# Top-32 attention and a squared-ReLU feed-forward on one core: 30 more idle products on TensorE, and new orders of the engines

## The chip, the cores and the metric

The kernel runs on one core of a Trainium2 chip. The metric is device time in microseconds (us) of one execution; less is better. The core has five engines with a queue each: TensorE (PE in the rows, PEld for its weight loads), VectorE (DVE), ScalarE (ACT), GpSimd (POOL) and SyncE (SP), which only issues DMAs here. Each executes its queue in order, and engines wait for each other by semaphores.

## What is computed

Eight batches, eight heads, 576 rows of 64. Each row of scores keeps its 32 largest entries, the rest get no weight; then a softmax and the product with v. The result, as 4608 rows of 512, goes through two products with a squared ReLU between them.

```python
scores = scale * np.matmul(q, k.transpose(0, 1, 3, 2))          # 8 x 8 x 576 x 576
kth = np.partition(scores, -top_k, axis=-1)[..., -top_k:-top_k + 1]   # top_k = 32
scores = np.where(scores >= kth, scores, -1000000000.0)
attn = np.exp(scores - np.max(scores, axis=-1, keepdims=True))
attn = attn / (np.sum(attn, axis=-1, keepdims=True) + 1e-09)
x = np.matmul(attn, v)            # then heads side by side: 4608 x 512
h = x @ w_in                      # 512 x 2048
g = np.maximum(h, 0.0) ** 2
out = g @ w_out                   # 2048 x 512
```

## The kernel before

The work is cut into 144 groups. A group is 128 rows of a pair of heads (or the last 64 rows of two pairs, the Z groups). Each goes through the same stages:

- TensorE multiplies q and k (`scores`, L870 in the rows, because all plain products go through one helper `mm`; transposes go through `tr`, L873). q and k were flipped before by five transposes each (`turned_`), and ScalarE copied them out of PSUM (L996).
- ScalarE copies the scores from PSUM to the tile `s` (`copied`, L1040), and VectorE folds them from PSUM (`fold`, L1118, three per group) into a list that holds the larger ones. GpSimd makes the complementary lists by two integer sums (`whole`, L1113).
- VectorE finds the threshold of each row by MAX8 and MATCH_REPLACE8 (L1165, L1180, L1160, L1183 for `kth`); for 71 of the groups ScalarE and GpSimd do a part of it (L1170, L1173).
- ScalarE makes the mask from `s` and `kth` (L1206, one activation for each of the two heads). TensorE turns the scores by transposes and adds the masks by products (`flip`: `turn`, then `mask`), and ScalarE exponentiates out of PSUM (`grow`, L1272).
- TensorE multiplies with v (`fav`, L1338), ScalarE drains it (L1375), GpSimd divides by the row sums (L1384), SP flips the result by DMA.
- For each chunk of 256 or 128 rows TensorE makes h (`fh`), ScalarE applies ReLU (L1430), GpSimd or ScalarE squares (L1445, L1448), TensorE multiplies with w_out (`fo`), ScalarE copies out (L1466) and SP stores.

GpSimd also issues 14 DMAs (`issue`, L1658 to L1660) that copy v, half a batch each, to a bf16 copy `vd` in memory; a 1x1 memset follows each. Loads of v for batches after the first read `vd`.

PSUM has eight banks: two areas of three (`large`: flips of q and k, scores, turns) and two single ones (`psum`: products with v, h, out, and idle products). Whoever takes an area waits until the last reader of its former content is done.

Two kinds of idle work are in TensorE's queue. An idle product (`t` in `times`, `fill=True`) multiplies a block of ones with 512 columns of ones into a `psum` bank; nobody reads it. A spare (`spare`, a negative number in the order) is three products of 128 columns added into an area that is about to be overwritten or read elsewhere.

The program makes all operations in a list, numbered as they are made, and `Plan.arrange` then puts them into an order written out by hand: `ORDER` has one string of numbers for each engine, and `SLOT` one digit for each tile, its place in its pool. Numbers below 89 are set-up, weight loads and casts and GpSimd's DMA issues (61, 63, ... 87); 89 to 2534 are idle products, of which the order names only a few; the rest follow from the groups. The semaphore waits follow from the order and the places.

```python
turns = {e: [int(x) for x in orders[e].split()] for e in ENGS}
place = {ops[x]: i for e in ENGS for i, x in enumerate(turns[e]) if x >= 0}
for t, s in zip(tiles, slots):
    if t.taker in place:
        t.slot = int(s)
```

Of the kernel before, what the change touches and what calls it, by code (L numbers as in the profile page):

```python
# [32 lines left out]
        "90 91 92 93 94 95 96 97 98 2541 2542 2543 2547 2574 2579 101 100 104 106 102 2613 2614 2617 2645 126 119 129 134 2683 136 135 2684 2577 2687 2750 "  # L33
        "2751 257 149 245 169 2605 2715 2607 2643 2754 209 3221 3222 274 2672 2783 153 2674 2713 2865 275 -5029 -5029 -5029 -5029 -5029 -5029 -5029 -5029 183 "
        "-5029 2895 240 283 2742 -5137 2924 -5041 2744 2781 210 2954 3286 3287 292 2810 2983 2891 294 2812 3017 2922 244 3048 190 148 3354 3355 241 204 2893 "
        "2950 3076 2952 -5157 219 2981 3107 3009 2817 276 2818 2820 2821 3135 3011 3419 3420 2824 2825 2827 2828 3044 3224 293 207 -5203 -5203 3252 256 278 "
        "2831 2838 2832 2839 3074 2841 2842 226 3289 3103 2834 2835 -5232 3046 -5232 -5232 3317 3133 2845 188 2848 2846 167 3357 3105 2847 2852 3162 2849 2851 "
        "2850 222 3164 3250 3385 3279 2855 2859 2856 2860 3422 3281 3315 2858 2857 3170 3450 3171 3344 2862 3173 3174 3532 3920 3921 3177 2861 3178 3562 3383 "
        "3184 3346 3185 3591 3180 195 3412 3181 3191 3192 3414 3448 3621 3187 3188 3985 3986 3194 -5409 3195 3650 3477 3198 3200 3201 3684 4053 4054 3205 "
        "-5409 3199 159 3204 3479 3558 3715 3589 3202 3560 3203 3743 3208 3210 3209 3212 3213 3617 3214 3215 3211 3648 3774 3619 3802 3491 3492 3484 3485 4118 "  # L40
        "3487 3488 3676 4119 3505 3494 3923 3506 3495 3711 3498 3508 3509 3499 3951 3678 3741 3501 3512 3514 3502 3988 3515 3713 3770 3519 3518 4016 3800 3513 "
        "3516 3772 3517 3829 4056 4084 3522 3525 3831 3526 3528 3949 3529 3978 3524 4588 4589 4121 3980 4014 3527 3523 3837 3838 4149 3840 3841 4043 3844 3845 "
        "3851 4045 4231 4082 3847 3852 3848 4261 4111 3854 3855 4290 3885 4113 4653 3887 3858 3888 3886 3859 4147 3890 3896 4654 3897 3891 4321 3892 3893 4176 "
        "3898 3899 3901 3903 3902 3904 4350 4384 3861 3862 3865 3866 4721 4178 4722 3867 3868 4257 4415 3870 4259 3869 3871 3875 3876 3877 4288 3881 3878 3872 "
        "4317 4443 3880 3882 4348 3879 3907 3909 4474 4786 4787 3910 3908 4319 4376 4502 3913 4378 3914 3912 3911 4411 4591 4183 4184 4441 4186 4187 4413 4619 "
        "4470 4190 4191 4656 4472 4500 4193 4197 4194 4198 4684 4204 4205 4200 4201 4724 4529 4207 4208 4211 4213 4752 4531 4212 4789 4221 4223 4214 4617 4215 "
        "4216 4228 4222 4218 4646 4227 4217 4682 4817 4225 4899 4226 4224 4537 4538 4540 4541 4544 4545 4711 4648 4929 4551 5287 5288 4552 4547 4548 4958 4558 "
        "4554 4555 4559 4750 4561 4562 4713 4779 4988 5352 4781 5353 4565 4566 4815 5017 4572 5420 5421 4571 4567 4844 5051 4925 4846 4568 4569 4570 4927 4956 "
        "5082 4575 5110 4577 4579 4582 4581 4578 4984 5141 4576 4580 5015 4986 4858 4859 5169 4851 4852 5043 4865 4866 4854 4855 5290 5485 5486 5045 4861 4862 "
        "5078 4872 4868 5318 4869 5108 4873 4875 4876 5355 5080 5137 4879 4881 4880 5383 4884 5139 5167 4882 4883 4885 4886 5196 5423 5316 5198 4889 4892 4894 "  # L50
        "5451 5955 5956 4890 4893 4896 4891 5345 5488 4895 5347 5381 5204 5205 5207 5516 5211 5208 5212 5598 5218 5219 5214 5215 5410 5221 5252 5254 5222 5253 "
        "5255 5628 5225 5226 5263 5264 5265 5266 5449 5257 5260 5258 5259 5412 5657 5478 5268 5269 5271 5228 5229 5270 5687 5242 5961 5962 5480 5243 5246 5716 "
        "5245 5248 5514 5244 5232 5249 5238 5543 5750 5237 5235 5997 5234 5247 5998 5239 5781 5233 5236 5624 5545 5274 5281 5810 5655 5278 5626 5279 5683 6003 "
        "6004 5841 5714 5685 5280 5277 5869 5276 5275 5742 5550 5551 5553 5554 5964 5744 5777 5564 5565 5557 5558 6006 5567 5808 5560 5561 6073 5568 5779 5837 "
        "5571 5572 5574 5575 6101 5867 5578 5579 5839 5580 6132 5581 5896 5582 5585 5584 5583 5588 5593 5595 5898 6160 5990 5594 5590 5591 5589 5592 6033 6194 "
        "5992 6656 6035 6657 5904 5905 5911 6099 6222 5907 5908 5912 6128 5914 5915 5918 6253 6130 6281 5919 5921 5922 6158 5925 5926 5928 5929 6363 6187 6041 "
        "6044 5932 6043 5934 5938 5935 6042 6391 5933 5939 6189 5936 5937 6422 6220 5942 5948 6046 5944 6047 5947 6048 6049 6450 6249 5945 5943 5946 5949 6251 "
        "6279 6662 6663 6052 6054 6055 6053 6484 6057 6059 6308 6060 6058 6063 6066 6512 6310 6065 6389 6064 6068 6543 6698 6699 6070 6069 6067 6418 6571 6704 "
        "6705 6420 6665 6448 6322 6323 6325 6707 6315 6326 6316 6477 6318 6319 6329 6742 6330 6510 6479 6332 6333 6772 6539 6336 6337 6339 6340 6806 6541 6353 "
        "6569 6343 6344 6348 6349 6347 6350 6346 6345 6836 6358 6598 6359 6354 6357 6355 6600 6691 6902 6734 6356 6360 6693 7385 7386 6932 6736 6966 6605 6606 "  # L60
        "6608 6609 6768 6612 6613 6615 6616 6799 6996 6770 6619 6620 7062 6801 6626 6627 6622 6623 6832 6629 6630 6633 6863 7092 6834 6634 6635 6636 6637 6640 "
        "6639 6638 6865 7126 6928 6643 6648 6649 6645 6644 6647 6930 6959 7156 6650 6646 6992 6961 6870 6871 6873 6872 6875 6877 6878 6876 7222 7023 6881 6884 "
        "6883 6886 6888 6889 6882 6887 7252 6994 7391 7392 6892 7025 6893 6898 7088 7286 6899 7428 7429 6894 6897 6896 6895 7316 7119 7090 7434 7435 7152 7394 "
        "7121 7030 7183 7031 7033 7035 7032 7038 7036 7037 7437 7041 7154 7044 7043 7248 7046 7048 7042 7049 7047 7504 7052 7055 7185 7053 7054 7250 7279 7534 "
        "7057 7281 7312 7058 7056 7059 7568 7343 7190 7193 7191 7192 7598 7314 7345 7421 7201 7203 7195 7196 7197 7198 7202 7204 7664 7206 7207 7208 7209 7212 "
        "7214 7213 7423 7215 7350 7352 7351 7353 7464 7694 7217 7466 7219 7216 7355 7218 7357 7358 7356 7530 7728 7361 7532 7362 7364 7363 7366 7368 7369 7367 "
# [1764 lines left out]
```

## Time and profile before

| | us |
|---|---|
| median of 3 runs (lowest, highest) | 744.44 (744.16, 746.62) |
| profiled execution | 745.29 |
| its span, first to last instruction | 743.5 |
| VectorE busy | 718.7 |
| ScalarE busy | 714.8 |
| TensorE busy with products | 698.1 |
| GpSimd busy | 685.1 |

The span is what the profiler saw from the first to the last instruction of the execution; the time lies 1.79 us above it. A busy time is the sum of what one engine executed, so the span less the busy time is what that engine idled in all. A mean granted clock of TensorE of 0.994 says that it was at its full level nearly throughout.

### The profile page before, as it was taken

The page shows a single profiled execution, that of the slowest core. Times are in us where ns is not written, and L with a number is a line of the kernel's source. Part 1 is how long each engine was busy: PE and PEld are TensorE (multiplying, and loading weights), DVE is VectorE, ACT ScalarE, POOL GpSimd, SP SyncE. Part 2 cuts the span into 40 slices and gives each one's busy share as a digit, 9 for nine tenths or more (in the row PEclk, how much of TensorE's full clock was granted, in tenths as well). Part 3 has the DMA queues.
Part 4 walks back from the last instruction along what each step waited for, and adds up shares of the span by engine and source line. Part 5 has one row for each costly group of instructions (what it writes and reads, how often), then busy time and mean ns, then how long its engine had stood idle before and what let it go on. Part 6 is the DMA issues. An engine that isn't in the chain of part 4 may idle for free.

```text
span 743.5 us, 27477 instructions
## 1 busy us (share of the span) xinstructions
PE 698.1 (94%) x10556; PEld 524.8 (71%) x10626; DVE 718.7 (97%) x3409; ACT 714.8 (96%) x1202; POOL 685.1 (92%) x526
## 2 busy tenths in 40 slices
PE   7787999999899999999999999999999999999997
PEld 3555766767677677767778677677677777777786
DVE  5999999999999999999999999999999999999996
ACT  4799999999999999999999999999999999999994
POOL 3799999999999999899999999999999999999981
PEclk9899999999999999999999999999999999999999
DMA  8765553354324441224332352204633032301101
GB/s 177 175 162 125 139 142 82 71 80 98 56 70 75 84 83 27 63 56 78 71 64 56 76 119 46 55 13 89 127 74 85 12 68 54 59 20 45 30 26 50
DMA packets 172729, 57.30 MB, mean 77 GB/s; under 512 B 157744, under 2 KB 164912, under 8 KB 172592
## 3 DMA queue, kind: packets, MB, share of 16 engines
q1 hardware_dynamic: 164528, 51.19, 29.8%
q0 software_dynamic: 7392, 4.13, 4.7%
q8 instruction: 84, 1.38, 0.8%
q14 instruction: 53, 0.43, 0.2%
q10 hardware_dynamic: 672, 0.16, 0.1%
HBM read 40.83 MB, written 13.57 MB: 73 GB/s over the span
## 4 chain that ended last, share of the span: by engine, by line
ACT 44%; PE 26%; DVE 19%; POOL 5%; issue 4%; DMA 1%; SPq 0%; ACTq 0%; POOLq 0%; DVEq 0%
PE ps L870 21%; ACT w L1206 12%; ACT s L1040 9%; ACT p L1272 9%; PE ps L873 6%; ACT g L1430 5%; DVE s L1118 4%; DVE s L1180 4%; DVE c L1165 4%; ACT s L1170 4%; DVE kth L1183 3%; DVE s L1160 3%; ACT qk L996 3%; POOL u L1113 2%; POOL s L1113 2%
## 5 line engine op out<-in xcount | busy, mean ns | idle before, releaser
L1113 POOL TENSOR_TENSOR u<-s 128x864 int32<-128x864 int32 x142 | 244.7, 1724 | 20.3 <-DVE s L1118 18.2
L1113 POOL TENSOR_TENSOR s<-s,u 128x864 int32<-128x864 int32 x142 | 242.8, 1714 | 3.5
L1206 ACT ACTIVATE w<-s,kth 128x576 bf16<-128x576 f32 x286 | 224.0, 834 | 1.9 <-DVE kth L1183 1.8
L1165 DVE MAX8 c<-s 128x8 f32<-128x140 f32 (+2 forms) x864 | 203.7, 265 | 0.1
L1118 DVE TENSOR_TENSOR s<-ps,s 128x288 f32<-128x288 f32 x432 | 192.4, 446 | 10.3 <-ACT s L1040 7.8
L870 PE MATMUL ps<-qk 64*128 64x192 f32 (+3 forms) x1280 | 179.7, 428 | 9.5 <-ACT p L1272 4.8
L1180 DVE MATCH_REPLACE8 s<-c,s 128x106 f32<-128x106 f32 (+2 forms) x722 | 181.5, 256 | 0.0
L1040 ACT COPY s<-ps 128x1152 f32<-128x1152 f32 (+1 forms) x145 | 168.2, 1161 | 5.2 <-PE ps L870 4.5
L1272 ACT ACTIVATE p<-ps 128x1152 bf16<-128x1152 f32 x143 | 169.1, 1182 | 3.1 <-PE ps L870 2.6
L870 PEld LDWEIGHTS ps<-qk 64*128 64x128 f32 (+1 forms) x1280 | 131.0, 176 | 38.1 <-ACT p L1272 15.3
L870 PE MATMUL ps<-wo,g 128*128 128x512 bf16 (+1 forms) x522 | 131.5, 373 | 9.1 <-issue 6.7
L870 PE MATMUL ps<-xt,win 128*128 128x256 bf16 (+1 forms) x1280 | 131.3, 252 | 1.3 <-ACT g L1430 0.4
L1183 DVE MAX8 kth<-s 128x8 f32<-128x296 f32 x288 | 129.3, 456 | 0.7 <-POOL s L1173 0.4
L1160 DVE MAX8 s<-s 128x8 f32<-128x288 f32 x288 | 126.5, 448 | 0.2 <-POOL s L1113 0.2
L873 PEld LDWEIGHTS ps<-ident,s 64*128 64x128 f32 x2592 | 95.6, 139 | 42.9 <-ACT w L1206 8.8
L873 PE MATMUL ps<-ident,s 64*128 64x64 f32 x2592 | 111.9, 228 | 11.4 <-ACT qk L996 3.8
L870 PEld LDWEIGHTS ps<-xt,win 128*128 128x128 bf16 x1280 | 98.1, 98 | 21.5 <-issue 4.1
L1445 POOL TENSOR_TENSOR g<-g 128x1024 bf16<-128x1024 bf16 x50 | 94.6, 1895 | 3.2 <-ACT g L1430 2.6
L1430 ACT ACTIVATE g<-ps 128x512 bf16<-128x512 f32 x140 | 86.9, 657 | 0.0
L870 PEld LDWEIGHTS ps<-wo,g 128*128 128x128 bf16 x592 | 48.8, 98 | 46.8 <-issue 5.5
L870 PEld LDWEIGHTS ps<-vb,p 128*128 128x128 bf16 (+1 forms) x1600 | 53.9, 100 | 23.3 <-ACT g L1430 5.1
L870 PE MATMUL ps<-steep_bf,w 64*128 64x64 bf16 x2584 | 66.7, 191 | 0.1
(90 smaller groups left out, 711.5 us busy)
## 6 DMA issues: line engine op xcount, KB each, us to landing
out_dram<-o SPq DMA_DIRECT2D x32, 256.0 KB, 2.3
rk<-in_k_dram SPq DMA_DIRECT2D x63, 128.0 KB, 2.5
rq<-in_q_dram SPq DMA_DIRECT2D x62, 128.0 KB, 2.6
s<-s SPq DMA_DIRECT2D x144, 32.0 KB, 1.9
g<-in_moe_w_in_dram SPq DMA_DIRECT2D x8, 512.0 KB, 4.5
g<-in_moe_w_out_dram SPq DMA_DIRECT2D x8, 512.0 KB, 4.4
vd<-in_v_dram POOLq DMA_DIRECT2D x14, 288.0 KB, 4.8
vb<-vd SPq DMA_DIRECT2D x56, 64.0 KB, 2.3
```

Of the source, the lines that this page charges most:

```text
L870: return pe.matmul(o, l, r, start=start, stop=stop, skip_group_check=True)
L873: return pe.matmul(o, i, ident, is_transpose=True, skip_group_check=True, **kw)
L1040: return pl.op("act", .14 + 2 * (c1 - c0) / 1200, pl.at("copy", tg - LEAD + 1), lambda: act.copy(at(st)[:, :, c0:c1], two(banks(ss)[:, FIR ...
L1113: return pl.op("gp", dur, prio, lambda: gp.tensor_tensor(o().bitcast(I32), x().bitcast(I32), y().bitcast(I32), op), **kw)
L1118: return dve(.36, lambda: vec.tensor_tensor(o(), two(banks(ss)[:, FIRST_AT + c:], SECOND, QUART), x(), ALU.max), r=[ss], **kw)
L1160: prev[i] = [dve(.0685 + HALF / 960, lambda i=i: vec.max(area(LIST, LIST + 8, i), area(LESS, LESS + HALF, i)), after=prev[i] + [low], hold ...
L1165: lambda i=i, t=t, span_=span_: vec.max(eighth(t, i), span_(i)),
L1180: lambda i=i, t=t, span_=span_: vec.match_replace(span_(i), eighth(t, i), span_(i), NEG), hold=[st])]
L1183: ks.append(chain(kth, i, prev[i], .0685 + (8 + HALF) / 960, lambda i=i: vec.max(eighth(kth, i), area(BIGS - QUART, LIST + 8, i)), hold=[st]))
L1206: masks[i:] = [pl.op("act", .77, pl.at("mask", tw + .8 * i), lambda i=i: act.activation(at(wt)[:, i, :], at(st)[:, i, 0:S], ACTF.Relu, bia ...
L1272: return act.activation(at(pt)[:, :, :].rearrange("p c (h q) -> p h c q", h=2), bass.AP(x.tensor, x.offset, [x.ap[0], [APART, 2], [64, 9], ...
L1430: return act.activation(at(g)[:, g0:g0 + 512], bank(hh)[:, 0:512], ACTF.Relu)
```

## The change

All of it is in the two constants. The order of TensorE names 81 idle products instead of 51: numbers 103, 105, 107 to 118, 120 to 125, 127, 128, 130 to 133, 137 and 138 within the first part, 89 and 99 far back. Some of the old ones (169, 183, 209, 244, 153, 148 and others) stand elsewhere. One spare of three products is replaced by another. Of the other operations the same ones are named: 557 of TensorE's 1128, 431 of ScalarE's 1059, 2309 of VectorE's 2687 and 184 of GpSimd's 508 stand at another place (by up to 14, 10, 45 and 14 places). GpSimd's DMA issues are among them: 63 stands ahead of 2693 (the second integer sum of the fifth group) instead of behind 2666 (a product of L1173); 65, 67 and 69 stand 6, 14 and 10 places earlier, 73 stands 10 later, the others by 1 to 11 in either direction. SP's order is the same. In `SLOT` 266 of 3990 places differ. The searched orders were made with a model that has the traced time of GpSimd's DMA issues; nothing of that model's constants is changed in the file.

In the cut diff, 2574 is the second flip of q, 2579, 2617, 2645, 2687, 2715 and 2754 are scores, 2613 and 2614, 2683 and 2684, 2750 and 2751 flips of q and k, 2577, 2605 and 2643 the first turns, 2607 a product with v.

```diff
@@ -30,191 +30,192 @@
 ORDER = {
     "pe": (
-        "90 91 92 93 94 95 96 97 98 2541 2542 2543 2547 2574 2579 101 100 104 106 102 2613 2614 2617 2645 126 119 129 134 2683 136 135 2684 2577 2687 2750 "
...
+        "90 91 92 93 94 95 96 97 98 2541 2542 2543 2547 2574 137 138 2579 101 100 104 106 102 2613 2614 131 132 133 2617 2645 126 119 129 134 127 128 130 2683 "
+        "136 135 2684 120 121 122 123 124 125 2577 2687 2750 2751 116 117 118 2605 2715 169 2607 183 2643 2754 3221 3222 274 2672 2783 209 2674 244 2713 2865 "
+        "153 148 -5029 -5029 -5029 -5029 -5029 -5029 -5029 -5029 -5029 2895 240 292 2742 111 112 113 114 115 -5041 2924 -5041 257 2744 2781 108 109 110 2954 "
...
+        "6994 7391 7392 6892 7025 6895 6893 7088 7286 6897 7428 7429 6894 6899 6896 6898 7316 7119 7090 89 99 7434 7435 7152 7394 7121 7030 7183 7033 7035 "
...
     "gp": (
-        "2539 1 2 7 5 3 4 6 8 9 11 10 16 25 28 15 13 21 23 26 19 20 22 2611 17 18 12 61 24 27 2576 14 2622 2623 2650 2651 2692 34 2693 2666 63 2720 36 2721 "
...
+        "2539 1 2 7 5 3 4 6 8 9 11 10 16 25 28 15 13 21 23 26 19 20 22 2611 17 18 12 61 24 27 2576 14 2622 2623 2650 2651 2692 34 63 2693 2666 2720 36 2721 "
...
@@ -231,8 +232,8 @@
...
 SLOT = (
-    "01010101010101010010101010010100000000000000001000000000000001010000000000011000000000000000001010000000000000100001000000100000000000101100"
...
+    "01010101010101010010101010010100000000000010001000001000000001010100000000001000000000000000001000000000000000100001010000000000000000100100"
...
```

## Rows read from the trace of the kernel before

**Rows 1.** The page of the profile: span, and busy time of each engine with its share of the span and its instructions.
```profile
span 743.5 us, 27477 instructions
PE 698.1 (94%) x10556; PEld 524.8 (71%) x10626; DVE 718.7 (97%) x3409; ACT 714.8 (96%) x1202; POOL 685.1 (92%) x526
```

**Rows 2.** Busy time by stretch. Columns: start and end, length, then busy us (instructions) of TensorE's products, its weight loads, VectorE, ScalarE and GpSimd, the granted clock, the share of the DMA engines, GB/s.
```profile
20.00:40.00 20.00, 16.35 (x186) 11.82 (x186) 18.35 (x89) 15.87 (x22) 15.46 (x13) 0.83 0.75 173
40.00:720.00 680.00, 648.09 (x9991) 489.40 (x10059) 671.92 (x3204) 676.87 (x1146) 656.84 (x473) 1.00 0.34 73
...
40.00:100.00 60.00, 50.75 (x815) 38.62 (x815) 59.88 (x286) 59.85 (x98) 58.53 (x47) 1.00 0.56 145
...
500.00:720.00 220.00, 213.01 (x3397) 163.32 (x3422) 216.25 (x1039) 218.12 (x376) 212.83 (x156) 1.00 0.27 58
```

**Rows 3.** The same view in steps of 2 us, with the same columns; the granted clock is the third number from the end.
```profile
22.00:24.00 2.00, 0.70 (x25) 0.70 (x26) 2.00 (x9) 1.27 (x2) 1.52 (x2) 1.00 0.93 209
24.00:26.00 2.00, 2.00 (x30) 1.51 (x24) 2.00 (x14) 1.13 (x1) 1.92 (x2) 0.65 1.06 321
26.00:28.00 2.00, 2.00 (x10) 1.51 (x9) 1.89 (x8) 1.83 (x3) 0.84 (x1) 0.50 0.22 48
...
32.00:34.00 2.00, 0.77 (x20) 0.65 (x20) 1.49 (x7) 2.00 (x3) 1.36 (x1) 1.00 1.07 262
34.00:36.00 2.00, 1.69 (x39) 1.69 (x41) 2.00 (x11) 1.59 (x7) 0.88 (x2) 0.71 0.74 160
36.00:38.00 2.00, 2.00 (x9) 1.33 (x6) 1.91 (x8) 1.05 (x2) 2.00 (x3) 0.50 0.86 253
...
52.00:54.00 2.00, 0.46 (x24) 0.35 (x19) 2.00 (x11) 2.00 (x5) 1.92 (x2) 1.00 1.00 250
```

**Rows 4.** TensorE's products in order of time, merged by line: start us, length us, engine, line, tiles and shape, count, and in brackets the idle time before them with what ended it. `qk` is the score product, `ident` a transpose, `ones_bf` an idle product, `steep_bf,w` the mask.
```profile
8.93 1.24 PE L870 MATMUL ps<-qk 64*128 64x192 f32 x8 [0.62 <-ACT qk L935]
...
14.94 2.21 PE L870 MATMUL ps<-qk 64*128 64x192 f32 x16 [1.21 <-ACT qk L996]
17.08 1.06 PE L870 MATMUL ps<-ones_bf 128*128 128x512 bf16 x4
19.30 0.86 PE L873 MATMUL ps<-ident,rq 128*128 128x128 f32 x5 [1.17 <-DVE s L1118]
...
23.30 0.78 PE L873 MATMUL ps<-ident,s 64*128 64x64 f32 x18 [1.97 <-ACT qk L996]
23.91 0.46 PE L870 MATMUL ps<-steep_bf,w 64*128 64x64 bf16 x18
24.18 1.93 PE L870 MATMUL ps<-qk 64*128 64x384 f32 x8
26.05 1.41 PE L873 MATMUL ps<-ident,rq 128*128 128x128 f32 x5
...
34.31 0.88 PE L873 MATMUL ps<-ident,s 64*128 64x64 f32 x18 [1.54 <-ACT w L1206]
34.97 0.69 PE L870 MATMUL ps<-steep_bf,w 64*128 64x64 bf16 x18
35.47 2.28 PE L870 MATMUL ps<-qk 64*128 64x192 f32 x8
37.68 0.61 PE L870 MATMUL ps<-ones_bf 128*128 128x512 bf16 x1
```

**Rows 5.** ScalarE in order of time, the same columns.
```profile
24.41 1.13 ACT L1272 ACTIVATE p<-ps 128x1152 bf16<-128x1152 f32 x1 [1.14 <-PE ps L870]
26.17 1.12 ACT L1040 COPY s<-ps 128x1152 f32<-128x1152 f32 x1 [0.63 <-PE ps L870]
...
35.71 1.13 ACT L1272 ACTIVATE p<-ps 128x1152 bf16<-128x1152 f32 x1 [0.41 <-PE ps L870]
37.78 1.12 ACT L1040 COPY s<-ps 128x1152 f32<-128x1152 f32 x1 [0.94 <-PE ps L870]
```

**Rows 6.** VectorE in order of time, the same columns.
```profile
33.62 0.46 DVE L1118 TENSOR_TENSOR s<-ps,s 128x288 f32<-128x288 f32 x1 [0.51 <-ACT s L1040]
...
35.13 0.45 DVE L1160 MAX8 s<-s 128x8 f32<-128x288 f32 x1
...
38.94 0.46 DVE L1118 TENSOR_TENSOR s<-ps,s 128x288 f32<-128x288 f32 x1 [1.03 <-ACT s L1040]
```

**Rows 7.** GpSimd in order of time, the same columns.
```profile
31.64 1.72 POOL L1113 TENSOR_TENSOR s<-s,u 128x864 int32<-128x864 int32 x1
35.12 0.69 POOL L1173 TENSOR_TENSOR s<-s 128x280 f32<-128x280 f32 x1 [1.76 <-ACT s L1170]
35.75 0.68 POOL L1659 DMA_DIRECT2D vd<-in_v_dram  x1
...
36.48 1.73 POOL L1113 TENSOR_TENSOR u<-s 128x864 int32<-128x864 int32 x1
```

**Rows 8.** Who waited for whom from 40 to 720 us: the waiting engine, tile and line, the one waited for, us in all, times, the longest.
```profile
DVE s L1118 <- ACT s L1040: 4.0, 14, 0.6
...
DVE kth L1183 <- POOL s L1173: 0.4, 2, 0.2
...
ACT p L1272 <- PE ps L870: 0.9, 3, 0.4
ACT av L1375 <- PE ps L870: 0.6, 1, 0.6
```

More of the change, by code (lines that the diff above doesn't have):

```diff
@@ L233 @@
 SLOT = (
-    "01010101010101010010101010010100000000000000001000000000000001010000000000011000000000000000001010000000000000100001000000100000000000101100"
-    "00000000010000000000000000001001000000000000100000000000000000110000000000000001100000000000000000000000000000000000000000000000000000000000"
+    "01010101010101010010101010010100000000000010001000001000000001010100000000001000000000000000001000000000000000100001010000000000000000100100"
+    "00000000000001000000000000000000000000000000000000000000000000000000001000000000110000000000000000000000000000000000000000000000000000000000"
     "00000000000000000000000000000000000000000000000000000000000000000000000000000000000000000000000000000000000000000000000000000000000000000000"
@@ L262 @@
-    "0512000006011100000101010000010011110101001201010010030012021101203110")
+    "00000000000000000000000000000000000000000000000000000000000000000000000000000000000010001000000011011000010111200120300001001111221401010500"
+    "10100010330610101001110010001112003000111100121002000003111100400100511111000160012110011000100010021102130010100000100201311010104140400101"
+    "51111000001016020210001010000511011111020000010010213110204001000001110020131000115110000060001100010011010202120010013001111141110050001116"
@@ new lines @@
+    "02120010101010011012103010011410511000203010000021111101130413020204101000100400050101160010001101110011001000100001111020131001112011001030"
+    "01014110101500020610000000100100000112011200000131112140000100010110210300001001021501001610011011503000212011000100002041201110300101111300"
+    "14010205000010001111020130101116110110100000011111002001213111000114000101151000060111000000201010000001010121130001104005010000011200011300"
+    "00001141204110215001010000103160101101000111150411000012001110001010121130001103101000140111150210006100210011010100100100102011103000011401"
@@ new lines @@
+    "02050010000001101201300001002001101106110000003121140300000110141000101112101200110003100014011110015001006010111000200110011010010110201300"
+    "01102100213000010040010151001100060102100010111100001201110000101112013100110010411210030010000000111502140111100151000010601010101000101001"
+    "11011010001110020010010301100001400110015011001001110100610001110001110101010000021001000011101003011001140000010151100100600010002000110003"
+    "13114041000100000100112110100100001002010121110101300100001411001005001100001010100612100100000010001110010020001010010111013011010040011001"
@@ L265 @@
+    "1512100016010100000101100100000010110000000201111011130002120001213110")
 class Pool:
```

11 lines of the change are left out of this document (removed), and 354 rows, old and new, of the table ORDER.

## The prediction

> **What bounds the kernel now.** I read the page's busy shares first, then the busy time by stretch, then the granted clock in steps of 2 us, then the time lines of the first 60 us, then the waits of the long middle. The reader is to see in the shares that four engines are nearly full [rows 1], so that no engine's total says much. The stretches say more [rows 2]. From 40 to 720 us ScalarE is busy 676.87 of 680 us and VectorE 671.92: they idle 3.13 and 8.08 us. From 20 to 40 us alone ScalarE idles 4.13 us and VectorE 1.65. The change alters no instruction of ScalarE or VectorE, only their order and what they wait for. So what it can win is idle time, of which the middle has very little. From 40 to 100 us neither engine has a gap to speak of (ScalarE 0.15, VectorE 0.12 us), so an advance won by both before 40 us arrives at 100 us whole; after that ScalarE, with the least idle time, sets the pace and VectorE has slack to follow.
>
> TensorE's granted clock says what is wrong before 40 us [rows 3]. [...] Ahead of the first fall TensorE was busy 0.70 of 2 us at 22; ahead of the second 0.77 at 32. But 0.46 of 2 us at 52 brought no fall.
>
> **The change part by part.** 30 idle products of 512 columns go into the order, and of the 51 that were there some are put elsewhere. At the upper level four of them take 1.06 us [rows 4], so one more costs 1.06 / 4 = 0.27 us at most, and 30 cost 8.0 us of TensorE against 45.4 us in which it idles (743.5 - 698.1) [rows 1]. Whether one costs time depends on its gap. The first new ones stand in waits that the rows show: 2 ahead of the scores at 8.93 us (0.54 of the 0.62 us in which they wait for a copy); 3 ahead of the scores at 14.94 (0.81 of 1.21); 3 behind the four that begin at 17.08, ahead of the flips at 19.30 (0.81 of 1.17); 6 ahead of the turn at 23.30, which waits for ScalarE to clear a PSUM area (1.62 of 1.97) [rows 4]. Those hide behind ScalarE and VectorE. Were the clock low there, the cover would be gone for the 6: an idle product then takes up to 0.61 [rows 4], 6 take at most 3.7, and the turn would start up to 1.7 us late with all of TensorE's queue behind it. [...] Of the later ones, 3 take the place of 4 old ones behind a pair of flips, and two of the old ones now stand around the products with the values, ahead of the gap of 1.54 us before 34.31 [rows 4]; 5 and 6 more stand ahead of score products and a turn between 50 and 65 us. By their PSUM places only the last of the five has to wait for a drain by ScalarE. Two stand far back, beside a turn in the last third, at 0.27 each.
>
> The gain is sought in the two slow spells. First: the score products at 24.18 took 1.93 us instead of 1.24, the flips at 26.05 took 1.41 instead of 0.86 [rows 4]. At the upper level the scores would end at 24.18 + 1.24 = 25.42, before ScalarE is through with the exponential (24.41 + 1.13 = 25.54) [rows 5], so its 0.63 us of idle time at 26.17 go. What the flips lose is followed by ScalarE's other work and counts nothing. Second: turn and mask products from 34.31 ended at 34.97 + 0.69 = 35.66, 1.35 us later, instead of 1.07 (23.30 to 23.91 + 0.46) [rows 4]; that is 0.28 of the 0.41 us of idle time at 35.71 [rows 5]. The scores ended at 35.47 + 2.28 = 37.75, 3.44 us behind the start of the turn, instead of 0.88 (24.18 - 23.30) + 1.24 = 2.12. The exponential then in work ends 1.07 + 0.05 + 1.13 = 2.25 behind that start, so the 0.94 us of idle time at 37.78 go as well. ScalarE wins 0.63 + 0.28 + 0.94 = 1.85 us. VectorE can win at most its 1.65 us, nearly all of it two waits of its folds for ScalarE's copies, 0.51 at 33.62 and 1.03 at 38.94 [rows 6]. As both are full from 40 to 100 us, the smaller decides: I take **1.6 us**, and keep 0 and 1.85 as ends.
>
> GpSimd's DMA issues: one takes 0.73 us until the next sum (36.48 - 35.75) [rows 7]; there are 14, and nearly all but the first get another place in GpSimd's queue. One shows the pattern: the second is moved from 35.75 to ahead of the sum at 31.64. That sum ends at 33.35 now, then at 34.08; VectorE first reads it at 35.13 [rows 6], and GpSimd idles 1.76 us before 35.12 [rows 7], so nothing is late, and the next sum can start 0.73 us earlier. Of VectorE's waits for GpSimd in the whole middle the largest sum is 0.4 us [rows 8], so there is next to nothing to win and I count 0; an issue put ahead of a sum that VectorE awaits would cost up to 0.73.
>
> The orders: VectorE's 2687 instructions are the same, 2309 of them at another place (by up to 45), ScalarE's by up to 10; SP's queue isn't touched, so loads and flips by DMA keep their turn. What a new order wins in the middle is bounded by ScalarE's 3.13 us of idle time; what it loses has no bound in a trace of the old one. The nearest row is the worst long stretch, 500 to 720 us, with 220 - 218.12 = 1.88 us idle [rows 2]: at that rate the 680 us would have 5.8, which is 2.7 us more. I take 0, between -3.1 and +2.7, and 0 for the tail, where the last groups' orders differ by a few places.
>
> **The sum.** The profiled execution took 745.29 us, 1.79 us more than its span. 745.29 - 1.6 = 743.7. It lies 0.85 us above the median of the runs shown, 744.44; so for the median 742.8 us.
>
> **The rivals.**
> The clock falls elsewhere (14%). 0.70 busy us of 2 at 22 were followed by a fall, 0.46 at 52 weren't [rows 3], so the work near a gap doesn't settle where the clock falls. With two such spells in other places before 60 us the gain is 0 and the time 744.4. Against it: the 6 products stand just where the first fall was prepared. [...]
>
> The new orders win in the middle too (32%): ScalarE loses 2.5 of its 3.13 us of idle time. For it: half of VectorE's 8.08 us are folds waiting for ScalarE's copies, 14 times, 4.0 us [rows 8], which is a matter of order. Against it: ScalarE's own largest waits there sum to 0.9 and 0.6 us, so 2.5 would have to come from many small ones. 744.4 - 1.6 - 2.5 = 740.3.
>
> The new order of VectorE stalls (16%, the other sign). Place: the folds (L1118), which wait for the copy of the scores; standing too early, a fold stops all that VectorE has behind it, and ScalarE's masks then wait for the thresholds. Price: 4.0 / 14 = 0.29 us each [rows 8]. VectorE has 8.08 - 3.13 = 4.95 us of slack on ScalarE, which 17 such waits use up. From 30 further waits in 144 groups on (8.7 - 4.95 = 3.8, less the 1.6 won) it decides for slower by 0.3%. With 35: 744.4 - 1.6 + 10.2 - 4.95 = 748.0; with one in every third group (48): 751.8.
>
> **How the numbers follow.** About 0.3%, 2.2 us, is what a measurement of this kernel can tell from no change. My forecast has 38%, with 741.7 to 744.2 as its own range. The faster rival has 32%, and a small part of the forecast's spread lies with it: faster 0.36. The rest of the forecast and the clock that falls elsewhere: same 0.48. Slower 0.16. The range for 8 in 10 goes from 739.8 (1.6 won at the head, 3.1 in the middle) to 746.4 (nothing won at the head, most of the 2.7 lost), and leaves out the slower rival.
>
> **What would show it.** Right: the clock at 1.00 from 20 to 40 us, score products of 1.24 us there, ScalarE's idle time from 20 to 40 us down from 4.13 to about 2.3, VectorE's from 1.65 to under 0.5; then ScalarE's idle time from 40 to 720 us within 1 us of 3.13. Wrong: a clock below 1.00 in another stretch, a turn that waits for nothing but an idle product ahead of it, or folds that wait more than 8 us in the middle. The prediction falls if the middle's idle time moves by more than the head's.

## The result and the profile after

The changed kernel takes 748.39 us (median of 12 runs, 747.78 to 754.28), the kernel before 744.75 us (12 runs, 744.16 to 746.62). The ratio is 1.0054, with a 95% interval of 1.0042 to 1.0065: slower by 0.5%, about 4 us. The profiled execution of after took 748.10 us, with a span of 746.2.

The busy time by stretch of the kernel after, with the columns of [rows 2]; its last stretch ends with the span:

```profile
20.00:40.00 20.00, 17.17 (x231) 11.45 (x232) 19.93 (x98) 17.59 (x24) 16.84 (x14) 1.00 0.81 186
40.00:720.00 680.00, 660.44 (x10046) 490.10 (x10044) 670.72 (x3197) 675.18 (x1145) 655.77 (x472) 1.00 0.34 72
720.00:746.20 26.20, 18.52 (x302) 15.32 (x302) 16.80 (x71) 12.58 (x24) 4.62 (x4) 0.91 0.11 37
```

Against [rows 2], the head did what the prediction said: the clock is 1.00, ScalarE idles 2.41 us instead of 4.13, VectorE 0.07 instead of 1.65. From 40 to 720 us ScalarE idles 4.82 us instead of 3.13 and VectorE 9.28 instead of 8.08. TensorE in order of time, kernel after, columns as in [rows 4] (lines are one higher than before's):

```profile
9.01 0.61 PE L871 MATMUL ps<-ones_bf 128*128 128x512 bf16 x2 [0.62 <-ACT qk L936]
9.55 1.24 PE L871 MATMUL ps<-qk 64*128 64x192 f32 x8
...
13.59 1.29 PE L871 MATMUL ps<-ones_bf 128*128 128x512 bf16 x3
...
21.20 2.41 PE L871 MATMUL ps<-ones_bf 128*128 128x512 bf16 x6
23.53 0.78 PE L874 MATMUL ps<-ident,s 64*128 64x64 f32 x18
...
24.41 1.25 PE L871 MATMUL ps<-qk 64*128 64x384 f32 x8
```

The scores at 24.41 take 1.25 us instead of 1.93. But the two products at 9.01 wait for the same copy as the scores behind them, which so begin 0.54 us after that wait ends, and the six at 21.20 take 2.41 us, not 1.62; the turn at 23.53 waits for nothing but them.

The end of the kernel needs a word, since the change has no text there. While the last products run, VectorE tests the thresholds of all groups (L1690 to L1717) and puts the outcome into one number, the flag (L1721). Every engine then reads the flag and jumps over a second programme:

```python
got["val"] = eng.value_load(flag[0:1, 0:1], min_val=0, max_val=P)
...
with eng.If(got["val"] > 0):
...
    em.emit(again, e, eng)
```

Behind the flag no engine computes anything; there are only the reading, the jump and the end of the programme. VectorE at the end, kernel after:

```profile
740.35 0.16 DVE L1715 TENSOR_SCALAR fone<-fone 128x2 f32<-128x2 f32 x1
740.80 0.16 DVE L1721 TENSOR_REDUCE flag<-ps 1x1 int32<-1x12 f32 x1 [0.29 <-PE ps L1719]
```

and the same instruction in the kernel before:

```profile
740.42 0.16 DVE L1720 TENSOR_REDUCE flag<-ps 1x1 int32<-1x12 f32 x1 [0.29 <-PE ps L1718]
```

So the flag comes 0.38 us later, and the span ends 746.2 - 740.80 = 5.40 us behind it instead of 743.5 - 740.42 = 3.08. Of the 2.7 us between the spans 2.3 lie where nothing is computed. The DMA queues of the two kernels, by kind, with packets, MB and share, show one difference there. First the kernel before, from 736.5 to 740.5 us and then to the end of its span at 743.5:

```profile
q14 instruction: 1, 0.01, 0.5%
...
q14 instruction: 4, 0.03, 3.8%
q8 instruction: 1, 0.02, 2.1%
```

Then the kernel after, from 736.5 to 740.9 us and then to 747, 0.8 us past the end of its span:

```profile
q8 instruction: 1, 0.02, 1.3%
...
q14 instruction: 5, 0.04, 1.9%
q8 instruction: 1, 0.02, 1.2%
```

Before fetches one packet of instructions on queue 14 ahead of the flag and four behind it. After fetches none ahead and five behind, of which the fifth starts at 746.49 us, 0.3 us after the last instruction has ended.

**How runs are compared below.** ScalarE's first copy (L928, columns as in [rows 5]) comes at 5.75 us in the first profiled execution of before and at 6.04, 6.81, 6.81 and 6.50 in four others of the same kernel: its wait, 2.43 us in the first and 3.49 in before_3, ends with TensorE's flips of the first loads. So I count the flag from that copy. "Exit" is from the flag to the end of the span.

| kernel | first copy | flag | flag - copy | exit | time, us | ratio to before, 95% |
|---|---|---|---|---|---|---|
| before, profiled | 5.75 | 740.42 | 734.67 | 3.08 | 745.29 | |
| before_again | 6.04 | 740.92 | 734.88 | 3.08 | 745.77 | |
| before_3 | 6.81 | 741.90 | 735.09 | 3.00 | 746.77 | |
| before_4 | 6.81 | 741.55 | 734.74 | 3.05 | 746.41 | |
| before_5 | 6.50 | 739.87 | 733.37 | 3.03 | 744.73 | |
| after | 5.83 | 740.80 | 734.97 | 5.40 | 748.39 | 1.0054 (1.0042 to 1.0065) |
| a_pad5 | 6.15 | 741.10 | 734.95 | 3.00 | 745.80 | 1.0011 (1.0002 to 1.0020) |
| a_pad1 | 6.57 | 741.23 | 734.66 | 5.87 | 748.96 | |
| a_hint300 | 6.56 | 741.52 | 734.96 | 5.48 | 748.77 | |
| b_pad123 | 6.49 | 739.92 | 733.43 | 5.38 | 747.86 | 1.0038 (1.0027 to 1.0049) |
| b_fills | 6.61 | 740.01 | 733.40 | 2.99 | 744.96 | 0.9999 (0.9990 to 1.0007) |
| b_fills_trim | 5.85 | 738.96 | 733.11 | 3.04 | 744.14 | 0.9985 (0.9976 to 0.9995) |
| a_nofill | 5.56 | 740.94 | 735.38 | 3.06 | 746.19 | 1.0022 (1.0009 to 1.0035) |
| a_tail_b | 6.14 | 743.11 | 736.97 | 2.99 | 747.94 | 1.0036 (1.0022 to 1.0050) |
| ab_706 | 6.20 | 740.24 | 734.04 | 3.06 | 745.39 | 1.0002 (0.9991 to 1.0013) |
| ab_343 | 5.79 | 739.29 | 733.50 | 3.01 | 745.15 | 0.9995 (0.9984 to 1.0005) |
| ab_106 | 6.81 | 740.07 | 733.26 | 3.03 | 744.89 | 0.9992 (0.9982 to 1.0002) |
| ab_106_trim | 6.16 | 739.04 | 732.88 | 3.06 | 744.09 | 0.9987 (0.9977 to 0.9997) |

Rows with a ratio give the median of 7 to 12 runs, the others a single one. The kernels were run in several groups; before's median was 744.57, 744.77, 744.84 and 745.15 us in them. Counted so, four kernels with after's orders and products give 734.97, 734.95, 734.96 and, in a_pad1, 734.66. The last shows the limit of this column. From the 31st exponential on, ten executions in the table run the same orders; from there to the flag four take 562.51 to 562.58 us and six 562.69 to 562.76. So an execution runs at one of two rates some 0.04% apart, worth some 0.25 us in the flag. It isn't TensorE's granted clock (before_4 and before_5 both have a mean of 0.998 and differ); why is open. The quicker rate is that of before_5, b_pad123, b_fills and b_fills_trim, and also of a_pad1, ab_343 and a_tail_b (191.14 to 191.16 us from the 23rd to the 61st exponential, where the five others with after's orders there take 191.23 to 191.25). Differences of a few tenths are therefore read from this column only between kernels at one rate, and the ratios, with some 0.7 to 1.1 us to either side, say how far they are borne out in time.

### The profile page after: what moved, and what is told of

Read it like the earlier page. It is cut to its first block, busy times and chain, and to the rows that moved or that the text cites. A ratio compares the mean times of both kernels' runs of the same rounds, so it can differ in the third digit from the quotient of the medians.

```text
span 746.2 us, 27592 instructions
## 1 busy us (share of the span) xinstructions
PE 713.4 (96%) x10656; PEld 525.6 (70%) x10656; DVE 719.3 (96%) x3409; ACT 714.1 (96%) x1202; POOL 684.7 (92%) x526
## 3 DMA queue, kind: packets, MB, share of 16 engines
q0 software_dynamic: 7392, 4.13, 4.7%
q8 instruction: 85, 1.39, 0.8%
## 4 chain that ended last, share of the span: by engine, by line
ACT 46%; PE 37%; DVE 11%; issue 3%; POOL 2%; ACTq 0%; POOLq 0%
PE ps L871 28%; ACT w L1207 12%; ACT p L1273 10%; ACT s L1041 9%; PE ps L874 8%; ACT g L1431 5%; ACT s L1171 4%; DVE s L1119 3%; DVE c L1166 2%; DVE s L1181 2%; ACT av L1376 2%; ACT qk L997 2%; DVE s L1161 1%; DVE kth L1184 1%; ACT g L1449 1%
## 5 line engine op out<-in xcount | busy, mean ns | idle before, releaser
L1207 ACT ACTIVATE w<-s,kth 128x576 bf16<-128x576 f32 x286 | 227.9, 840 | 2.1 <-DVE kth L1184 2.0
L1166 DVE MAX8 c<-s 128x8 f32<-128x92 f32 (+2 forms) x864 | 204.7, 264 | 0.1
L871 PE MATMUL ps<-qk 64*128 64x192 f32 (+3 forms) x1280 | 177.9, 425 | 6.0 <-ACT p L1273 2.9
L1181 DVE MATCH_REPLACE8 s<-c,s 128x92 f32<-128x92 f32 (+2 forms) x722 | 181.4, 255 | 0.0
L871 PE MATMUL ps<-wo,g 128*128 128x512 bf16 (+1 forms) x592 | 144.7, 375 | 1.0 <-ACT av L1376 0.4
L871 PE MATMUL ps<-vb,p 128*128 128x65 bf16 (+1 forms) x1600 | 62.9, 194 | 3.9 <-POOL vb L1000 1.2
```

The lines of the kernel that those rows point to most:

```text
L871: return pe.matmul(o, l, r, start=start, stop=stop, skip_group_check=True)
L1166: lambda i=i, t=t, span_=span_: vec.max(eighth(t, i), span_(i)),
L1181: lambda i=i, t=t, span_=span_: vec.match_replace(span_(i), eighth(t, i), span_(i), NEG), hold=[st])]
L1207: masks[i:] = [pl.op("act", .77, pl.at("mask", tw + .8 * i), lambda i=i: act.activation(at(wt)[:, i, :], at(st)[:, i, 0:S], ACTF.Relu, bia ...
```

## The experiments

**The exit.** Two theories: "block", my conjecture, that VectorE's jump had come to lie at the edge of a fetched block of its instructions, and "order", that the new order of the work makes the exit long. The page counts 3409 instructions of VectorE in both kernels; what the new stream has less are five waits, which it doesn't count (the trace itself holds 110 and 105 of them up to the flag).

a_pad5:

```diff
+PAD = {2545: 5}
...
+            for _ in range(PAD.get(o.seq, 0) if at and e == "dve" else 0):
+                self.pad()
             for k, v in o.waits:
                 eng.wait_ge(self.sem(k), v)
...
+    def em_pad():
+        c = next(blank_col)
+        return vec.memset(blank_row[:, c:c + 1], 0.0)
```

> The kernel after, with five tiny writes (one element each, to a row nobody reads) put into VectorE's instructions where it idles ahead of its first copy. Theory 'block': after the flag is read, 5.2 us pass to the end of the span where before has 2.9, because VectorE's stream got five instructions shorter and its last branch came to lie at the edge of a fetched block of instructions; with five more it lies where before's lies, the stretch from flag to end falls back to 2.9 us, and the time is 748.4 - 2.3 = 746.1 us (745.8 to 746.4). Rival 'order': the long exit comes from the new order of the work itself (a late check, a late store); five idle writes change nothing, 748.1 to 748.7 us and 5.2 us from flag to end.

Measured: 745.80 us and an exit of 3.00 us, as "block" says (the expectations count from the reading of the flag, 0.2 us behind its start: 2.9 and 5.2). Queue 14 from 736 to 741.1 us and then to 745, past the end of the span at 744.1, a_pad5:

```profile
q14 instruction: 1, 0.01, 0.6%
...
q14 instruction: 4, 0.03, 2.2%
```

The packet ahead of the flag is back. The flag stays where it was (734.95 against 734.97 us behind the first copy): the whole gain is the exit's.

b_pad123, the reverse. In after VectorE runs 124 and 128 counted instructions in two stretches between packets of queue 14, at 626.45, 653.25 and 679.70 us; two other packets of that queue lie between them (columns as in [rows 2], VectorE's the third busy time):

```profile
626.45:653.25 26.80, 25.69 (x454) 20.35 (x449) 26.16 (x124) 26.80 (x54) 25.89 (x21) 1.00 0.25 50
653.25:679.70 26.45, 26.05 (x428) 19.62 (x427) 26.45 (x128) 26.12 (x49) 25.91 (x20) 1.00 0.10 25
```

I took 128 for such a block, an estimate from these two stretches; 123 writes are one block less the five.

```diff
+PAD = {2545: 60, 2549: 24, 8114: 27, 8134: 12}
```

> The kernel before, with 123 such writes spread over VectorE's idle stretches (60 ahead of its first copy, 24 ahead of its first fold, 27 and 12 at about 730 and 733 us), so that its last branch lies one block of 128 instructions beyond the place of after's. Theory 'block': the exit from flag to end grows from 2.9 to 5.2 us though no order changes, 744.7 + 2.3 = 747.0 us (746.7 to 747.8 with what the writes themselves may cost). Rival 'order': the exit stays 2.9 us and the time 744.7 to 745.5.

Measured: 747.86 us, exit 5.38 us, with every order as in before. The time lies 0.1 us above the expected range, the exit where it was expected. The packets of queue 14 from the flag to 746 us, past the end of the span at 745.3, b_pad123; from 730 us to the flag there was none:

```profile
q14 instruction: 5, 0.04, 2.6%
```

a_pad1 and a_hint300 ask whether it is the place of the jump or something that happens to go with it.

```diff
+PAD = {2545: 1}
```

> The kernel after with one such write instead of five. Theory 'block': the edge lies between after's branch and the few instructions that read the flag ahead of it; one instruction more leaves the branch within 0.1 us of the edge, so flag to end stays near 5.1 us. Rival 'count': any change of VectorE's count cures it, flag to end 2.9 us.

```diff
-    HINT = 600
+    HINT = 300
```

> The kernel after with the branch announced 300 us ahead of the planned end instead of 600, on every engine; nothing else moves, and VectorE's branch stays where it lies. Theory 'block': flag to end stays 5.2 us, 748.1 us. Rival 'announcement': the long exit comes from where the announcement stands; moved, flag to end falls to 2.9 us, 745.8 us.

Measured: exits of 5.87 and 5.48 us, 748.96 and 748.77 us (one run each), and in both five packets behind the flag and none in the 5 us ahead of it. So neither another count alone nor another place of the announcement shortens the exit; what goes with the long exit in all four kernels that have it is the missing packet. "Order" is refuted.

The views leave the jumps out, but the traces hold them, and they settle where the time goes. Counted with its waits, VectorE's stream up to the flag, its jump (start behind the start of the flag, us) and the time from the end of the jump to VectorE's next instruction are:

| kernel | instructions up to the flag | jump behind the flag | jump to next instruction |
|---|---|---|---|
| the 14 with a short exit | 3521 to 3523 | 1.09 | 0.56 |
| after | 3516 | 1.47 | 3.58 |
| a_hint300 | 3516 | 1.47 | 3.62 |
| a_pad1 | 3517 | 1.46 | 4.01 |
| b_pad123 | 3644 = 3516 + 128 | 1.47 | 3.58 |

No other engine is late: their closing instructions start 1.5 to 1.8 us behind the flag in the four executions with a long exit as in the others (SyncE's at 2.55 in a_tail_b). The 0.4 us ahead of VectorE's jump lie directly before it in after, a_hint300 and b_pad123, and one instruction earlier in a_pad1, which has one instruction more ahead of the jump. The jump is the fourth instruction behind the flag, so they lie at one place of the counted stream, ahead of its 3520th instruction, in after, a_hint300 and a_pad1, and ahead of the 3648th, 128 further on, in b_pad123. What VectorE waits for behind the jump isn't shown: the four packets behind the flag start 2.1 to 2.7 us behind it in either case.

**The products alone.** b_fills puts 28 of the 30 added products among before's orders:

```diff
-... 2547 2574 2579 101 100 104 106 102 2613 2614 2617 2645 126 119 129 134 2683 136 135 2684 2577 2687 2750 2751 257 ...
+... 2547 2574 137 138 2579 101 100 104 106 102 2613 2614 131 132 133 2617 2645 126 119 129 134 127 128 130 2683 136 135 2684
+120 121 122 123 124 125 2577 2687 2750 2751 116 117 118 257 ...
...
-... 2742 -5137 2924 ... 210 2954 3286 3287 292 ...
+... 2742 111 112 113 114 115 -5137 2924 ... 210 108 109 110 2954 3286 3287 103 105 107 292 ...
```

> The kernel before with its orders on all engines, and 28 of the added idle products put where the kernel after has them among the same products up to about 39 us. Theory: the head's gain (clock 1.00 from 20 to 40 us) is 1.6 us and the old orders keep it to the end: 744.7 - 1.6 = 743.1 us (742.7 to 743.6), ScalarE idle 40 to 720 within 0.5 us of before's 3.13. Rival: whatever the order, later waits take back about 1 us of the lead: 744.0 to 744.6 us, ScalarE idle 40 to 720 near 4.8.

Measured: 744.96 us, no gain. Yet its flag comes 733.40 us behind the first copy, 1.27 us earlier than in the profiled execution of before, some 0.25 of it the rate. The two readings agree only if most executions of before are better than the profiled one. a_nofill asks the same of the new orders: it is a_pad5 without the 30 products.

```diff
-... 2574 137 138 2579 ... 2614 131 132 133 2617 ...
+... 2574 2579 ... 2614 2617 ...
...
-... 7090 89 99 7434 ...
+... 7090 7434 ...
```

> The kernel after with the five writes of a_pad5, without its 30 added idle products; all orders and PSUM places else as after. Theory 'not typical': the products win little in a usual execution, 745.8 + 0 to 0.4 = 745.8 to 746.2 us. Rival 'the head's 1.6 us': without them the clock falls between 24 and 40 us and the time is 745.8 + 1.6 = 747.4 us (747.0 to 747.8).

Measured: 746.19 us, 0.4 more than a_pad5, and a flag 0.43 us later: "not typical". The clock did fall in it, to 0.55 and 0.60 in the four us from 24, and that cost no more.

**What a usual execution of before is.** Four more profiled executions of the unchanged kernel.

> The kernel before once more, unchanged, for a second profiled execution. Most timed executions of before show a mean granted clock of 0.998, the profiled one 0.994. Theory 'not typical': the stretches at clock 0.50 to 0.71 between 24 and 40 us belong to that execution; a usual one has clock 1.00 from 20 to 40 us, ScalarE idle there near 2.4 us instead of 4.13, a span near 742.7, and so nothing that added products could win. Rival 'typical': the clock falls there again, by 1.5 us or more of lost full-speed time.

> The kernel before, unchanged, a third profiled execution. Theory 'not typical': an execution whose mean granted clock is 0.997 or more shows no stretch below 1.00 between 20 and 40 us, and its flag comes 733.6 us after ScalarE's first copy, as in b_fills, against 734.9 and 735.1 in the two profiled ones with clock 0.994 and 0.992; one of 0.995 or less shows such stretches. Rival 'elsewhere': at 0.997 and more too the clock falls between 20 and 40 us, and the mean differs by what is lost in the exit.

> The kernel before, unchanged, a fourth profiled execution, with the same two readings: at a mean clock of 0.997 or more no fall between 20 and 40 us ('not typical'), or a fall there all the same ('elsewhere').

> The kernel before, unchanged, a fifth profiled execution, with the same two readings: at a mean clock of 0.997 or more no fall between 20 and 40 us ('not typical'), or a fall there all the same ('elsewhere').

Measured: before_again, with mean clock 0.992, had falls at 14 to 20, 24 to 30 and 34 to 40 us, which went against "not typical". before_3 (0.995) had one at 22 to 28 and one at 54 to 58. before_4 and before_5 (both 0.998) had none before 40 us and one behind 52. before_5, columns as in [rows 3]:

```profile
24.00:26.00 2.00, 1.83 (x40) 1.51 (x36) 2.00 (x14) 1.30 (x2) 1.92 (x2) 1.00 1.04 295
...
36.00:38.00 2.00, 2.00 (x12) 1.23 (x11) 2.00 (x10) 1.99 (x3) 2.00 (x2) 1.00 0.89 208
52.00:54.00 2.00, 1.57 (x11) 1.09 (x11) 2.00 (x12) 1.94 (x5) 2.00 (x4) 0.92 0.82 247
54.00:56.00 2.00, 2.00 (x33) 1.89 (x33) 2.00 (x12) 2.00 (x3) 2.00 (x3) 0.50 0.48 125
56.00:58.00 2.00, 1.56 (x35) 1.19 (x31) 2.00 (x10) 0.92 (x2) 2.00 (x2) 0.73 0.29 59
```

Its flag comes 733.37 us behind the first copy, where 733.6 was expected counted to the reading of the flag, 0.2 us later: it is the flag of b_fills. Of 95 timed executions of before in four groups, 58 had a mean clock of 0.997 or more (21 of 30, 9 of 13, 21 of 35, 7 of 17); their medians in the groups are 744.5 to 744.7 us, those of the others 745.0 to 746.5. before_4 lost its time otherwise: its first exponential comes 19.31 us behind the first copy, b_fills' 18.50, and its flag 734.74. Its first eight score products, at 7.35 us, took 2.29 us where before_5's took 1.24, at a recorded clock of 1.00; why isn't settled.

The stretches at half speed of [rows 3] are thus real, but by the mean clocks some three executions in five don't have them at that place.

**What the orders cost.** a_tail_b is a_pad5 with the last 49 operations of VectorE in before's order:

```diff
 "dve"
-... 8101 8162 8164 8096 8043 8098 8156 8100 8165 8102 8106 ...
+... 8101 8096 8098 8154 8043 8100 8102 8155 8158 8156 8106 ...
```

> The kernel after with the five writes, and the last 49 of VectorE's operations (last selections, folds and checks) in the order that before has. Theory: the new order leaves more of the checks to the end, where the flag waits for them; with the old one the flag comes about 1.0 us earlier, 745.1 us (744.8 to 745.5), 1.0 below the run with five writes alone. Rival: the flag is bound by the last products, and the order of the checks moves it by under 0.3 us: 745.8 to 746.3.

Measured: 747.94 us, wrong on both counts; the flag is 2.0 us later than in a_pad5. VectorE's waits at the end of a_tail_b:

```profile
734.13 0.29 DVE L1543 TENSOR_TENSOR g<-g 128x256 bf16<-128x256 bf16 x1 [1.22 <-ACT g L1540]
736.12 0.96 DVE L1543 TENSOR_TENSOR g<-g 128x512 bf16<-128x512 bf16 x3 [1.50 <-ACT g L1540]
743.11 0.16 DVE L1746 TENSOR_REDUCE flag<-ps 1x1 int32<-1x12 f32 x1 [1.81 <-PE ps L1744]
```

VectorE's old order stands among new orders of ScalarE and TensorE and waits for them. One engine's order can't be judged alone. So the next kernels change over from after's orders to before's on all engines at one time, at a point where both have done the same work; PSUM places change over with them. The diff is one seam for each engine. ab_343 and ab_106 leave out the two far products (89 and 99) as well, ab_106 also one old one (293). VectorE's seam for ab_706:

```diff
 "dve"
-... 7995 8049 8000 7884 7997 8050 8020 7999 8002 ...
+... 7995 8049 8000 7884 7997 8020 8050 8002 7999 ...
```

> The same, changing over at about 706 us, so that the last 106 operations of VectorE and what the other engines do beside them stand in before's order. Theory 'late checks': the flag comes 1.54 us later than in b_fills while the exponential at 725 us comes only 0.44 us later, so 1.0 to 1.1 us are lost in the order of the last 35 us: 745.8 - 1.0 = 744.8 us (744.5 to 745.2). Rival 'owed work': VectorE comes to 706 us with 1 us of work more to do, whatever the order behind it: 745.6 to 746.0 us.

> The same, changing over to the old orders at about 343 us. Theory 'later orders': the lead over b_fills there is only 0.2 to 0.3 us, and is kept: 744.7 us (744.4 to 745.0), about 0.5 above the change-over at 106 us and 1.1 below the new orders throughout. Rival 'head': 745.8 us as before.

> The kernel after with the five writes, and from about 106 us on the orders and PSUM places of before on every engine (the work done by then is the same in both). Counted from ScalarE's first copy, the new orders are 0.8 us ahead of the old ones with the products (b_fills) at the exponential at 95 us. Theory 'later orders': what the new orders lose, they lose behind that point, and the old ones keep the lead to the flag: 744.96 - 0.8 = 744.2 us (743.8 to 744.6). Rival 'head': the lead of ScalarE hides work that VectorE still owes, and the flag comes as with the new orders throughout, 745.8 us (745.4 to 746.2).

Measured: 745.39, 745.15 and 744.89 us, each a little above its expected range (by 0.2, 0.15 and 0.3 us). ab_706, ScalarE's first copy and the flag (columns as in [rows 5]):

```profile
6.20 0.27 ACT L954 COPY qk<-ps 128x128 f32<-128x128 f32 x1 [2.88 <-PE ps L899]
```

```profile
740.24 0.16 DVE L1746 TENSOR_REDUCE flag<-ps 1x1 int32<-1x12 f32 x1 [0.29 <-PE ps L1744]
```

That flag is 0.91 us earlier than a_pad5's, at the same rate: the order of the last 35 us costs 0.9 us, as "late checks" said, though the median fell by 0.4 only (the ratio by 0.0009, 0.7 us). Between 106 and 706 us the new orders lose 734.04 - 733.26 = 0.78 us, both flags at the slower rate. How this divides at 343 us isn't shown, since ab_343's flag is at the quicker rate. Nor is all of it the orders' for sure: the two far products, which ab_343 and ab_106 leave out, take 0.38 and 0.39 us of TensorE at 620.42 and 620.86 us in ab_706, 614 us behind the first copy. ab_706's exponential 596 us behind the first copy comes 0.14 us ahead of ab_343's, the one at 618 us 0.53 us behind it. A run without these two alone wasn't made.

"Later orders" holds in kind: no median is at the 745.8 of "head" and of "owed work". ab_106's median missed the expected 744.2 by 0.7, for its lead over b_fills at 95 us, 0.8 us, is that of ScalarE. From 106 us on both run the same orders, and at 110 us VectorE ends the same instruction only 0.43 us earlier in ab_106; the flag is VectorE's. It leads by 0.14 us at the end, which with the rate allowed for is the same 0.4.

**The products that cost.**

```diff
-... 2574 137 138 2579 ... 2684 120 121 122 123 124 125 2577 ...
+... 2574 2579 ... 2684 120 121 122 2577 ...
```

> As ab_106 without five of the 30 added products: the two behind which the score products at 8.9 us waited 0.6 us (137, 138), and the last three of the six before the turn at 23.3 us, which outlast its gap by 0.2 us. Theory: the head is 0.2 to 0.3 us shorter and the clock stays at 1.00, 743.9 us, 0.2 to 0.3 below ab_106. Rival: the clock falls at 24 us for want of them, no gain or 0.3 us more than ab_106.

> b_fills (the old orders with 28 of the added products) without the five that ab_106_trim leaves out. Theory: the five cost 0.4 us wherever they stand, so 744.96 - 0.4 = 744.5 us (744.2 to 744.8), equal to a usual execution of before: the products are worth nothing there, and the 0.5 us by which ab_106_trim is faster still (744.1) come from the new orders of the first 106 us. Rival: trimmed products alone win what ab_106_trim wins, 743.9 to 744.2 us.

Measured: 744.09 and 744.14 us. Five products less win 0.8 us in both medians, where 0.2 to 0.3 and 0.4 were expected, and by the second run's rival: the trimmed products on the old orders win all that ab_106_trim wins. The flags, each pair at one rate, move by 0.38 and 0.29 us only. TensorE in b_fills_trim, columns as in [rows 4]:

```profile
9.03 1.24 PE L885 MATMUL ps<-qk 64*128 64x192 f32 x8 [0.62 <-ACT qk L950]
...
20.91 1.29 PE L885 MATMUL ps<-ones_bf 128*128 128x512 bf16 x3
22.95 0.78 PE L888 MATMUL ps<-ident,s 64*128 64x64 f32 x18 [0.75 <-ACT qk L1011]
...
23.82 1.25 PE L885 MATMUL ps<-qk 64*128 64x384 f32 x8
```

The turn again waits for ScalarE and not for products, and the clock holds at 1.00 from 20 to 58 us all the same. b_fills_trim is faster than both kernels, by 0.15% (0.05 to 0.24%) than before. In its group ten of the 17 executions of before had a mean clock under 0.997; against the other seven (median 744.46) it wins 0.3 us, as its flag against before_5's says.

## Why the prediction was wrong, step by step

**The exit (no term).** The sum ended at the span's last work; no term and no rival dealt with the 3.08 us behind the flag. They became 5.40, 2.3 of the 4 us lost: VectorE's five waits less put its jump five instructions earlier in its stream, and with five writes in their place the exit was 3.00 us (a_pad5). A term couldn't have been sized from the trace of before, but the risk could have been named: the change moves waits, some waits are instructions of their own (110 and 105 in the two traces), and a jump lies behind them. In the four long exits VectorE's next instruction comes 3.58 to 4.01 us behind its jump, in the fourteen short ones, which take the same jump, 0.56; why the place of the jump does that isn't shown. That the instructions come in blocks of 128 stays an estimate: in after queue 14 moves 0.43 MB in 52 packets, 8 KB each, queue 8 1.39 MB in 85, 16 KB each; VectorE ran 124 and 128 counted instructions between packets of queue 14, and the long exit came again with 128 instructions more ahead of the jump.

**The head (1.6 us).** The mechanism was right: from 20 to 40 us ScalarE idles 1.72 us less in after, VectorE 1.58. For the execution that was read the size was somewhat too large: the 21st exponential comes 118.91 us behind the first copy there, 117.89 in b_fills and 117.61 in b_fills_trim, the same orders at full clock, so 1.0 and 1.3 us. (The flags are 1.27 and 1.56 us apart, some 0.25 of it the rate.) The step that failed is the last of the sum: "It lies 0.85 us above the median of the runs shown, 744.44; so for the median 742.8". The gain was carried over to a median that mostly had it. A usual execution, before_5, has its fall of the clock where it costs little, and its flag leaves 0.26 us to b_fills_trim and nothing to b_fills. The first rival, a clock that falls elsewhere, agrees with five executions of the unchanged kernel, whose falls lie at different places between 14 and 60 us (clocks of 0.74 and 0.50 in the four us from 14 in before_again, 0.92 and 0.50 in the four from 52 in before_5); but the rival applied it to after, whose clock was 1.00 from 10 to 60 us, and it bore on the trace of before. What a fall hangs on isn't shown.

**The price of a product (0.27 us, cover in the gaps).** Mis-sized. The two ahead of the scores at 8.93 us were to fill "0.54 of the 0.62 us in which they wait for a copy"; they waited for that copy themselves (9.01 us above). The six ahead of the turn were to take 1.62 us and took 2.41. At the same clock three at 13.59 took 1.29 us, 0.43 each, where four of [rows 4] took 0.27 each. By the PSUM places in the source the three go to one place and the four to two in turn; that this is the reason wasn't tested. The two far back were priced at 0.27 each but don't stand in the sum; they take 0.38 and 0.39 us, and what they cost in the end wasn't tested. The five that were dropped are worth 0.3 to 0.4 us in the flag and 0.8 in the medians.

**The middle (0, between -3.1 and +2.7).** ScalarE's idle time rose by 1.69 us and VectorE's by 1.20, in the range but on the other side than the larger rival. From 106 to 706 us the new orders, with the two far products, lose 0.8 us.

**The tail (0).** Failed: 0.9 us. "The last groups' orders differ by a few places" overlooked that an instruction's own length can hang on its place. VectorE's last 120 instructions are the same ones in both kernels, but they keep it busy for 26.82 to 26.86 us in the five executions with after's order there and for 25.86 in ab_706 (25.82 in before); it idles 4.2 to 4.4 us among them in all of these. 0.6 of the 1.0 us is one test of eight columns, in after (with a squaring by GpSimd beside it) and in before:

```profile
723.24 1.89 POOL L1446 TENSOR_TENSOR g<-g 128x1024 bf16<-128x1024 bf16 x1 [1.48 <-ACT g L1431]
724.15 1.01 DVE L1691 TENSOR_TENSOR signs<-signs,c 128x8 f32<-128x8 f32 x1
...
729.44 0.37 DVE L1690 TENSOR_TENSOR signs<-signs,c 128x8 f32<-128x8 f32 x1
```

In all five executions the test ends 0.03 us behind that squaring. That it waits for GpSimd is likely, but wasn't tested.

**The rivals.** The one on the other side had the right engine and sign: VectorE's folds. Its measure, kernel after from 40 to 720 us, answers to [rows 8]:

```profile
DVE s L1119 <- ACT s L1041: 6.6, 23, 0.5
```

That is 9 more waits, not the 30 from which it should decide, so as priced it didn't happen. Nor did the slack of 4.95 us that it granted VectorE on ScalarE show: the kernel ends with VectorE's tests, and of ScalarE's lead of 0.8 us in ab_106 the flag kept what VectorE had of it, some 0.4. "ScalarE, with the least idle time, sets the pace and VectorE has slack to follow" was the wrong reading of [rows 2] for this kernel.

**The account.** Against before_5, after's flag is 1.60 us later and its exit 2.37 us longer: 3.97 us, where the ratio says 4.0 and the medians 3.64. Some 0.25 of the 1.60 is the rate and no loss. Along the chain of kernels the 1.60 are 0.91 (last 35 us), 0.78 (106 to 706 us, the two far products included) and 0.38 (five products), less 0.49 that the other products and the first 106 us of new orders win (0.7 with the rate allowed for): 1.58. The chain adds up by construction, each step being the difference of two flags, so it says how the loss divides and is no check of the sum.

**What would have shown it.** Clock, scores and idle time in the head came as listed; so did one of the wrong signs, a turn (23.53) that waits for nothing but idle products. ScalarE's idle time in the middle was to stay within 1 us of 3.13, and rose by 1.69: that sign pointed the right way, to a loss as large as the head's gain.

## What to carry to other kernels

A term that comes from the granted clock of one execution needs a second execution, or the clocks of the timed runs, before it is subtracted from a median. When instructions are reordered ahead of a jump, compare the stretch behind the last work and the packets of the instruction queues first: 2.4 us were lost there, and five idle writes won them back. Judge a new order by the engine whose work ends the kernel, on all engines at once, and put no filler behind the very wait that its successor has.

## What was not expected of the hardware

Where the jump stands in VectorE's stream is worth 2.3 to 2.9 us of exit: 2.99 to 3.08 us in fourteen executions (3521 to 3523 instructions up to the flag), 5.38 to 5.87 in four (3516, 3517 and 3644). With the orders unchanged, 123 idle writes bring the long exit about. In the profiled execution they cost nothing else: b_pad123's flag is at 733.43, before_5's at 733.37. Its median lies 3.3 us above before's, 0.9 more than the exit; its timed executions had mean clocks of 0.991 to 0.996, before's in that group 0.994 to 0.999.

The same test of eight columns takes VectorE 0.37 to 0.39 us in thirteen executions and 1.01 to 1.02 in the five in which it runs beside a squaring of 1.9 us by GpSimd.

The first copy of the kernel varies by 1.25 us (5.56 to 6.81) from execution to execution, more than most of the differences sought here, and the whole execution by some 0.04% in rate.
